# Soft-capped attention into two feed-forward layers on one Trainium2 core: moving the decode of the first weight units behind each pair's reciprocal, two first-half columns first, unread products and another load order in the first pair

## The chip, the cores and the metric

The kernel runs on one core of one Trainium2 chip. The metric is device microseconds of an execution; the time before is 618.9 us, the median of three runs (618.87 to 618.9). About 0.2% of that, 1.2 us, is what a measurement of this kernel can tell from no change.

Engines as the profile names them: PE is TensorE's matmul, PEld its weight load, DVE VectorE, ACT ScalarE, POOL GpSimd, SP SyncE (here it only issues DMAs).

## The reference

```python
scores = cap * np.tanh((1 / np.sqrt(64)) * np.matmul(q, k.transpose(0, 1, 3, 2)) / cap)   # cap = 30
attn = np.exp(scores - np.max(scores, axis=-1, keepdims=True))
attn = attn / (np.sum(attn, axis=-1, keepdims=True) + 1e-09)
x = np.matmul(attn, v)            # 2 batches, 12 heads, 448 tokens, head size 64 -> 896 x 768
h = x @ w_in                      # 768 -> 2048
g = h * (1.0 / (1.0 + np.exp(-1.702 * h)))
x = g @ w_out                     # 2048 -> 768
xn = x / np.sqrt(np.mean(x * x, axis=-1, keepdims=True) + 1e-06) * rms_g
g, val = xn @ w_gate, xn @ w_val  # 768 -> 1536 each
out = (g * (1.0 / (1.0 + np.exp(-g))) * val) @ w_out2
```

All inputs and outputs are float32. The kernel computes the large products with every operand split into a rounded part and a remainder, and three matmuls for each product.

## The kernel before

**Attention.** The 24 heads are worked two at a time, as 12 pairs. `attention()` has a loop over p from 0 to 12 (L436). Iteration p starts the scores of pair p+1 and ends the work of pair p-1, so that three pairs are under way. For a pair PE does seven transposes of q and k (`turn`, L250), the scores in three chunks of 128 keys (`scores`, L292) and a last one of 64 keys for both heads (`scores_last`, L302), the product with v (`outputs`, L324 and L329) and the sums of the exponentials (`sums`, L356). ACT does tanh and exp of each chunk (`exps`, L314 and L315; the last chunk writes `tl`). DVE splits the transposed q and k (`split_kq`, L269 and L270), adds two chunks of exponentials (`add_two`, L343), copies the output `z` (L335), takes the reciprocal of the sums (L361), and, for a pair that is up to four iterations older, multiplies `z` by the spread reciprocal and splits it into the input `x` of the first layer (`normal`, L383, L388, L395). The last pair's copy of `z` and its rounded part are ACT's (L337, L390).

The order on each engine is the order of the code: the program is issued by hand, and an engine works its list from the top. A tile that is used in rotation makes its next writer wait for its last reader. Three things use the two-deep PSUM tile `v` in turn: the last scores chunk of pair p, the outputs of pair p-1, the sums of pair p-1. So the outputs of pair p wait until the reciprocal of pair p-1 has read its sums, and the sums of pair p-1 wait until ACT's tanh of the last chunk of pair p has read that tile.

**First pair.** Six products of ones (L411, `WARM`) run while q and k of the first pair arrive. They are written to a `v` tile that nobody reads. The eight transposes of pair 0 follow (`tq`, `tk`), ACT and DVE split them (L277, L279), and the scores of pair 0 start. SP issues the loads in the order k of pair 0, v of pair 0, k and q of pairs 1 and 2, v of pairs 1 and 2. ACT issues q of pair 0.

**Weights.** The weights come in 68 units of six blocks of 128 x 128 and are loaded as raw words (`load_to`, L113). Each is decoded into a rounded part and a remainder in eight steps: on ACT `square`, `sign`, `mask` (L125, L129, L133), on DVE `mid`, `top`, `low` (L137, L143, L149), then `high_part` on ACT (L158) and `low_part` on DVE (L163, after `high_part`). `low` of a unit also issues the load of the unit three further on. During the attention a table, `plan`, says in which iteration which step of units 0 to 3 is issued. A call in the middle of the iteration issues one ACT step (two in iteration 11). A second call, ahead of `sums`, issues the rest, DVE's among them:

```python
if p >= 4:
    normal(p - 4)
...
decode(p if p < NPR else p + 1)
...
if p >= 1:
    sums(p - 1)
```

**First layer.** `ffn1` computes a column: one weight unit times one of two token ranges, of 384 (`b` = 0) or 512 tokens (`b` = 1), 18 matmuls (L549 to L551). The `b` = 0 columns read only the first batch's pairs, 0 to 5. The `b` = 1 columns read both batches', pair 11 in their last three matmuls. The list `order` starts with `HEAD` = 3 columns of `b` = 0 (units 0, 1, 2), then the same units' `b` = 1. `slots` says which decode steps are issued beside each column. The spread of the last pair's reciprocal (`spread_product`, L376, into `b`) comes behind the first column.

Of the kernel before, what the change touches and what calls it, by code (L numbers as in the profile page):

```python
# [18 lines left out]
def attn_moe_kernel(  # L19
# [157 lines left out]
    def attention():  # L177
        with ExitStack() as actx:
# [66 lines left out]
            def turn(p):  # L245
# [10 lines left out]
                else:  # L256
                    t = [ps_s.tile([128, 2, 512], F32, tag="s", name="tq")[:, 0],
                         ps_t.tile([128, 2, 512], F32, tag="t", name="tk")[:, 0]]
                    for j in range(2):
                        for c in range(NC + 1):  # L260
                            flip(t[j][:, c * 128:(c + 1) * 128], c + (NC if j == 0 else 0))
                turned[p] = t
# [141 lines left out]
            load_v(0)  # L404
            load_k(1)
            load_q(1)
            load_v(1)

            warm = ps_v.tile([128, 512], F32, tag="v", name="v")
            for _ in range(WARM):  # L410
                nc.tensor.matmul(out=warm[:, 0:S], lhsT=ones, rhs=xA[0][:, 0, 0:S], start=True, stop=True)  # L411

            plan = {
                3: [(square, 0)], 4: [(sign, 0)], 5: [(mask, 0)], 6: [(square, 1), (mid, 0)],
                7: [(sign, 1), (top, 0), (low, 0)], 8: [(mask, 1)], 9: [(high_part, 0), (mid, 1)],
                10: [(square, 2), (top, 1), (low_part, 0)], 11: [(sign, 2), (low, 1)],
                12: [(high_part, 1), (mask, 2), (low_part, 1)],
                13: [(square, 3), (sign, 3), (mid, 2)],
                14: [(top, 2), (low, 2)],
                15: [(high_part, 2), (low_part, 2), (mask, 3), (mid, 3), (top, 3), (low, 3)],  # L420
            }

            def decode(p, n=9):
                for _ in range(min(n, len(plan.get(p, ())))):
                    run(*plan[p].pop(0))
# [11 lines left out]
            for p in range(NPR + 1):  # L437
                if p < NPR:
# [9 lines left out]
                    decode(p, 2 if p == NPR - 1 else 1)  # L448
# [7 lines left out]
                if p < NPR:  # L456
                    add_two(p)
                else:
                    decode(NPR)
# [6 lines left out]
                if p == NPR - 1:  # L466
                    late = ps_t.tile([128, 2, 512], F32, tag="t", name="late")
                    spread_product(p - 2, late[:, 0])
                    normal(p - 2)
                decode(p if p < NPR else p + 1)  # L470
# [6 lines left out]
                if p == NPR:  # L477
                    decode(NPR + 2)
                    spread_product(p - 2, late[:, 1])
                    normal(p - 2)  # L480

# [8 lines left out]
            decode(NPR + 3)  # L490
            return spread_product, norm_mul, norm_hi, norm_lo

    def rest(spread_product, norm_mul, norm_hi, norm_lo):
        with ExitStack() as fctx:
# [95 lines left out]
            HEAD = 3  # L590
# [4 lines left out]
            for c in range(NC1):  # L595
# [9 lines left out]
                if c == 0:  # L605
                    slots[0] = [(op, 3) for op in DVE_OPS] + [(op, 4) for op in ACT_OPS] + slots[0]
# [3 lines left out]
                for n, (i, b) in enumerate(order):  # L610
                    last = ()
                    if c == 0 and n == 0:
                        later(lambda: spread_product(q3, bank()))
                        later(*[lambda fn=fn: fn(q3) for fn in (norm_mul, norm_hi, norm_lo)])
                        last = (lambda: load_to(5), load_g, lambda: [run(op, 3) for op in DVE_OPS])
# [243 lines left out]
```

## Time and profile before

| what | value |
|---|---|
| median of three runs | 618.9 us |
| the profiled execution | 618.96 us |
| its span, first to last instruction | 617.2 us |
| PE busy | 605.4 us (98%), 3371 matmuls |
| DVE busy | 450.7 us (73%) |
| ACT busy | 398.7 us (65%) |
| POOL busy | 72.0 us (12%) |

The profiled execution's own time is 1.8 us more than its span; that part is outside the first and last instruction. Busy shares are means over stages that have different limits. The chain that ended last is PE for 93% of the span and DVE for 4%, so what matters is where PE waits, and for whom.

### The profile page before, as it was taken

How to read it: one execution, taken by the hardware profiler on the slowest of the kernel's cores; microseconds unless marked ns; L12 is line 12 of the kernel's file. 1: busy time of each engine (PE TensorE's matmuls, PEld its weight loads, DVE VectorE, ACT ScalarE, POOL GpSimd, SP SyncE). 2: the span in 40 equal slices, each digit the busy share in tenths (PEclk: the TensorE clock that was granted, in tenths of full speed). 3: DMA queues.
4: the chain of work that ended last, by engine and by line, in shares of the span. 5: the costliest groups of instructions: out<-in, count | busy, mean ns of one | idle time of the engine just before them, and what ended most of it. 6: DMA issues, size and time to landing. Idle time of an engine off the chain costs nothing.

```text
span 617.2 us, 8577 instructions
## 1 busy us (share of the span) xinstructions
PE 605.4 (98%) x3371; PEld 515.0 (83%) x3371; DVE 450.7 (73%) x548; ACT 398.7 (65%) x532; POOL 72.0 (12%) x94
## 2 busy tenths in 40 slices
PE   7999998999999999999999999999999999999997
PEld 5555554588888898999888988899988899999997
DVE  1668888869875553666778899997388897688842
ACT  5899989379876465777766675766456574356400
POOL 3232322000000000000022201300022200022100
PEclk9899999999999999999999999999999999999999
DMA  5675541234434323333333432334132343333012
GB/s 134 137 195 134 138 107 30 64 106 150 155 104 152 111 94 103 102 104 102 104 109 112 134 106 103 103 102 154 52 102 103 106 151 104 102 103 103 0 73 107
DMA packets 85079, 67.17 MB, mean 109 GB/s; under 512 B 39040, under 2 KB 82358, under 8 KB 85040
## 3 DMA queue, kind: packets, MB, share of 16 engines
q1 hardware_dynamic: 80448, 64.27, 34.3%
q0 software_dynamic: 3632, 2.13, 1.3%
q8 instruction: 26, 0.43, 0.3%
q10 hardware_dynamic: 960, 0.23, 0.2%
q14 instruction: 13, 0.11, 0.1%
HBM read 63.80 MB, written 2.78 MB: 108 GB/s over the span
## 4 chain that ended last, share of the span: by engine, by line
PE 93%; DVE 4%; issue 1%; DMA 1%; ACT 0%; ACTq 0%; DVEq 0%
PE b L551 22%; PE b L550 22%; PE b L549 22%; PE b L753 14%; PE s L292 4%; PE v L324 4%; PE v L356 2%; PE t L250 1%; PE v L302 1%; PE v L329 1%; DVE rs L361 1%; DMA kq<-in_q 1%; DVE x L269 1%; DVE x L270 1%; DVE z L383 0%
## 5 line engine op out<-in xcount | busy, mean ns | idle before, releaser
L551 PE MATMUL b<-x,ring 128*128 128x512 f32 (+1 forms) x480 | 174.2, 363 | 0.0
L550 PE MATMUL b<-x,ring 128*128 128x512 f32 (+1 forms) x480 | 174.1, 363 | 0.0
L549 PE MATMUL b<-x,ring 128*128 128x512 f32 (+1 forms) x480 | 174.0, 362 | 0.0
L549 PEld LDWEIGHTS b<-x,ring 128*128 128x128 f32 x480 | 90.1, 188 | 10.4 <-issue 0.7
L550 PEld LDWEIGHTS b<-x,ring 128*128 128x128 f32 x480 | 90.1, 188 | 9.8
L551 PEld LDWEIGHTS b<-x,ring 128*128 128x128 f32 x480 | 90.1, 188 | 9.4
L137 DVE SCALAR_TENSOR_TENSOR dec<-raw,dec 128x768 uint32<-128x768 uint32 x68 | 69.7, 1025 | 26.7 <-ACT dec L133 25.3
L753 PE MATMUL b<-ring,uA 128*128 128x384 f32 x504 | 87.8, 334 | 0.0
L753 PEld LDWEIGHTS b<-ring,uA 128*128 128x128 f32 x504 | 87.4, 188 | 0.0
L143 DVE SCALAR_TENSOR_TENSOR dec<-raw,dec 128x768 uint32<-128x768 uint32 x68 | 73.1, 1076 | 1.1
L551 PE MATMUL b<-g,ring 128*128 128x384 f32 (+1 forms) x192 | 70.0, 365 | 0.0
L550 PE MATMUL b<-g,ring 128*128 128x384 f32 (+1 forms) x192 | 69.9, 364 | 0.0
L549 PE MATMUL b<-g,ring 128*128 128x384 f32 (+1 forms) x192 | 69.6, 362 | 0.0
L163 DVE TENSOR_TENSOR ring<-dec,ring 128x768 fp32r<-128x768 f32 x68 | 66.8, 983 | 3.6 <-ACT ring L158 3.6
L158 ACT ACTIVATE ring<-dec 128x768 fp32r<-128x768 f32 x68 | 56.7, 834 | 19.6 <-DVE dec L149 11.4
L149 DVE SCALAR_TENSOR_TENSOR dec<-raw,dec 128x768 uint32<-128x768 uint32 x68 | 64.9, 954 | 1.4
L129 ACT ACTIVATE dec<-dec,edge 128x768 f32<-128x768 f32 x68 | 63.4, 932 | 1.0
L125 ACT ACTIVATE dec<-raw 128x768 f32<-128x768 f32 x68 | 61.0, 896 | 0.6 <-DVE ring L163 0.5
L133 ACT ACTIVATE dec<-dec 128x768 f32<-128x768 f32 x68 | 57.3, 842 | 1.4
L721 POOL TENSOR_TENSOR a<-a,gg 128x512 f32<-128x512 f32 (+1 forms) x18 | 29.6, 1646 | 188.6 <-DVE gg L714 184.2
L724 ACT ACTIVATE uA<-a 128x512 fp32r<-128x512 f32 (+1 forms) x24 | 13.9, 579 | 46.3 <-POOL a L721 34.5
L314 ACT ACTIVATE tt<-s,tsc 128x896 f32<-128x896 f32 x36 | 35.9, 996 | 7.2 <-PE s L292 7.0
(102 smaller groups left out, 675.2 us busy)
## 6 DMA issues: line engine op xcount, KB each, us to landing
raw<-in_moe_w_out SPq DMA_DIRECT2D x20, 768.0 KB, 4.2
raw<-in_moe_w_in SPq DMA_DIRECT2D x16, 768.0 KB, 4.6
raw<-in_moe_w_gate SPq DMA_DIRECT2D x12, 768.0 KB, 4.3
raw<-in_moe_w_val SPq DMA_DIRECT2D x12, 768.0 KB, 4.2
raw<-in_moe_w_out SPq DMA_DIRECT2D x8, 512.0 KB, 3.7
out<-oacc SPq DMA_DIRECT2D x6, 384.0 KB, 2.3
raw<-in_moe_w_out SPq DMA_DIRECT2D x8, 256.0 KB, 3.4
r<-recs POOLq DMA_DIRECT2D x9, 224.0 KB, 7.9
```

The source lines that it names most:

```text
L125: nc.scalar.activation(out=f(d), in_=f(r[:, :, 1]), func=AF.Square, scale=2.0 ** 15)
L129: nc.scalar.activation(out=f(d), in_=f(d), func=AF.Sign, bias=edge)
L133: nc.scalar.activation(out=f(d), in_=f(d), func=AF.Relu, scale=2.0 - 2.0 ** -23)
L137: nc.vector.scalar_tensor_tensor(out=d, in0=hi, scalar=3, in1=d, op0=ALU.logical_shift_left, op1=ALU.bitwise_and)
L143: nc.vector.scalar_tensor_tensor(out=d, in0=hi, scalar=0xC0000000, in1=d, op0=ALU.bitwise_and, op1=ALU.bitwise_or)
L149: nc.vector.scalar_tensor_tensor(out=d, in0=lo, scalar=29, in1=d, op0=ALU.logical_shift_right, op1=ALU.bitwise_or)
L158: nc.scalar.activation(out=t[:, 0], in_=f(dec_t[w][0]), func=AF.Copy)
L163: nc.vector.tensor_tensor(out=t[:, 1], in0=f(d), in1=f(t[:, 0]), op=ALU.subtract)
L549: nc.tensor.matmul(out=wide(o, b), lhsT=w0, rhs=x0, start=first, stop=False)
L550: nc.tensor.matmul(out=wide(o, b), lhsT=w0, rhs=x1, start=False, stop=False)
L551: nc.tensor.matmul(out=wide(o, b), lhsT=w1, rhs=x0, start=False, stop=last)
L753: nc.tensor.matmul(out=os_[t][n][:, 0:HW], lhsT=uA[xi][:, i, tok], rhs=w[:, wi, n * HW:(n + 1) * HW], start=(i == 0 and xi == 0 and wi == ...
```

## The change

Five edits:

1. `plan` becomes `plan_a`, ACT's steps, issued in the middle of an iteration, and `plan_d`, DVE's steps. `plan_d` is issued at the end of the iteration, behind `sums` and so behind the pair's reciprocal.
2. Unit 2 keeps only its three ACT steps in the attention, and these move to iteration 12, beside unit 3's three ACT steps. Its DVE steps and its `high_part` and `low_part` move behind the first column of the first layer (`first`).
3. `HEAD` is 2, so that two columns of `b` = 0 come first instead of three.
4. The unread product of ones is also issued once behind the first transpose of pair 0 and twice behind the last.
5. The loads of k and q of pairs 1 and 2 are issued ahead of the load of v of pair 0.

In iterations 11 and 12, `normal(p - 2)` also moves behind the reciprocal.

```diff
@@ turn(p), for p == 0
                         for c in range(NC + 1):
                             flip(t[j][:, c * 128:(c + 1) * 128], c + (NC if j == 0 else 0))
+                            if j == 0 and c == 0:
+                                warm_up(1)
+                    warm_up(2)
                 turned[p] = t
@@ attention()
-            load_v(0)
             load_k(1)
             load_q(1)
+            load_v(0)
             load_v(1)
...
-            plan = {
-                3: [(square, 0)], 4: [(sign, 0)], 5: [(mask, 0)], 6: [(square, 1), (mid, 0)],
-                7: [(sign, 1), (top, 0), (low, 0)], 8: [(mask, 1)], 9: [(high_part, 0), (mid, 1)],
-                10: [(square, 2), (top, 1), (low_part, 0)], 11: [(sign, 2), (low, 1)],
-                12: [(high_part, 1), (mask, 2), (low_part, 1)],
-                13: [(square, 3), (sign, 3), (mid, 2)],
-                14: [(top, 2), (low, 2)],
-                15: [(high_part, 2), (low_part, 2), (mask, 3), (mid, 3), (top, 3), (low, 3)],
+            def warm_up(times):
+                for _ in range(times):
+                    nc.tensor.matmul(out=warm[:, 0:S], lhsT=ones, rhs=xA[0][:, 0, 0:S], start=True, stop=True)
+
+            warm_up(WARM)
+
+            plan_a = {
+                3: [(square, 0)], 4: [(sign, 0)], 5: [(mask, 0)], 6: [(square, 1)], 7: [(sign, 1)],
+                8: [(mask, 1)], 9: [(high_part, 0)], 11: [(high_part, 1)],
+                12: [(square, 2), (sign, 2), (mask, 2), (square, 3), (sign, 3), (mask, 3)],
             }
+            plan_d = {
+                6: [(mid, 0)], 7: [(top, 0)], 8: [(low, 0)], 9: [(mid, 1)],
+                10: [(top, 1), (low, 1), (low_part, 0)], 11: [(low_part, 1)],
+            }
...
-                    decode(p, 2 if p == NPR - 1 else 1)
+                    decode(plan_a, p)
                     exps(p, 2, s2)
...
                     spread_product(p - 2, late[:, 0])
-                    normal(p - 2)
-                decode(p if p < NPR else p + 1)
                 if p >= 2 and p - 2 < NPR - 3:
                     spread(p - 2)
                 if p >= 1:
...
                 if p == NPR:
-                    decode(NPR + 2)
                     spread_product(p - 2, late[:, 1])
+                if p >= NPR - 1:
                     normal(p - 2)
+                decode(plan_d, p)
@@ rest()
-            HEAD = 3
+            HEAD = 2
...
-                    slots[0] = [(op, 3) for op in DVE_OPS] + [(op, 4) for op in ACT_OPS] + slots[0]
+                    first = (
+                        [(op, 2) for op in (*DVE_OPS, high_part, low_part)]
+                        + [(op, 3) for op in DVE_OPS] + [(op, 4) for op in ACT_OPS] + slots[0]
+                    )
+                    slots[0] = []
...
-                        last = (lambda: load_to(5), load_g, lambda: [run(op, 3) for op in DVE_OPS])
+                        last = (
+                            lambda: [run(*some) for some in first], lambda: load_to(5), load_g,
+                        )
```

Line numbers move in the changed kernel: up to L261 they are the same, then three more (L361 becomes L364), in the first layer's columns five more (L549 becomes L554), and behind them eleven more.

**DVE in iteration 7.** `rs` is the reciprocal's result, `dec` a unit under decoding (here unit 0, `top` at L143 and `low` at L149), `x<-t` the split of the next transposes. Before:

```order
L395 TENSOR_TENSOR x1_67<-z_610,x0_66 128x448
L143 SCALAR_TENSOR_TENSOR dec_478<-raw_372,dec_478 128x768
L149 SCALAR_TENSOR_TENSOR dec_478<-raw_372,dec_478 128x768
L361 RECIPROCAL rs_921<-v_908 128x224
L269 CAST x_961<-t_953 128x896
```

And in the changed kernel:

```order
L398 TENSOR_TENSOR x1_67<-z_613,x0_66 128x448
L364 RECIPROCAL rs_920<-v_907 128x224
L143 SCALAR_TENSOR_TENSOR dec_481<-raw_375,dec_481 128x768
L272 CAST x_961<-t_953 128x896
L273 TENSOR_TENSOR x_961<-t_953,x_961 128x896
```

The two decode steps stood ahead of the reciprocal. Now the reciprocal is first, one decode step follows it, and the other has moved to the next iteration.

**DVE in iterations 10 and 11.** `dec_762` and `dec_765` are unit 1, `ring` the decoded unit; L163 is `low_part` of unit 0. Before:

```order
L395 TENSOR_TENSOR x1_67<-z_890,x0_66 128x448
L143 SCALAR_TENSOR_TENSOR dec_762<-raw_456,dec_762 128x768
L163 TENSOR_TENSOR ring_1036<-dec_478,ring_1036 128x768
L361 RECIPROCAL rs_1176<-v_1163 128x224
L149 SCALAR_TENSOR_TENSOR dec_762<-raw_456,dec_762 128x768
L343 TENSOR_TENSOR ts_1205<-tt_1178,tt_1181 128x896
```

And in the changed kernel:

```order
L398 TENSOR_TENSOR x1_67<-z_893,x0_66 128x448
L364 RECIPROCAL rs_1175<-v_1162 128x224
L143 SCALAR_TENSOR_TENSOR dec_765<-raw_459,dec_765 128x768
L149 SCALAR_TENSOR_TENSOR dec_765<-raw_459,dec_765 128x768
L163 TENSOR_TENSOR ring_1039<-dec_481,ring_1039 128x768
L346 TENSOR_TENSOR ts_1207<-tt_1182,tt_1185 128x896
```

Here too the reciprocal has moved ahead of the decode steps, and three of them now stand between it and the sum of two chunks (`ts`).

**ACT in iteration 11.** `tt` and `tl` are the exponentials of pair 11, and `ring<-dec` is `high_part` of unit 1. Before, behind the first two chunks of the pair:

```order
L129 ACTIVATE dec_1124<-dec_1124,edge_61 128x768
L314 ACTIVATE tt_1195<-s_1184,tsc_60 128x896
L315 ACTIVATE tt_1195<-tt_1195,capt_59 128x896
L314 ACTIVATE tl_1202<-v_1198,tsc_60 128x448
L315 ACTIVATE tl_1202<-tl_1202,capt_59 128x448
L158 ACTIVATE ring_1244<-dec_762 128x768
L133 ACTIVATE dec_1124<-dec_1124 128x768
```

And in the changed kernel:

```order
L158 ACTIVATE ring_1195<-dec_765 128x768
L317 ACTIVATE tt_1197<-s_1188,tsc_60 128x896
L318 ACTIVATE tt_1197<-tt_1197,capt_59 128x896
L317 ACTIVATE tl_1204<-v_1200,tsc_60 128x448
L318 ACTIVATE tl_1204<-tl_1204,capt_59 128x448
L125 ACTIVATE dec_1247<-raw_649 128x768
L129 ACTIVATE dec_1247<-dec_1247,edge_61 128x768
```

Unit 2's `sign` (L129) has gone from this place, and `high_part` of unit 1, which reads what DVE's `low` (L149) of unit 1 writes, now stands ahead of the pair's last two chunks instead of behind them.

## Rows read from the trace of the kernel before

**Rows 1.** The page's first part: busy time, share of the span, instructions of each engine

```profile
PE 605.4 (98%) x3371; PEld 515.0 (83%) x3371; DVE 450.7 (73%) x548; ACT 398.7 (65%) x532; POOL 72.0 (12%) x94
```

**Rows 2.** Windows by stage; behind the window: length, busy us of each engine, PEclk, DMA

```profile
74.00:118.50 44.50, 40.92 (x348) 20.32 (x342) 38.28 (x49) 36.57 (x44) 8.73 (x13) 1.00 0.28 76
140.00:350.00 210.00, 210.00 (x1044) 188.75 (x1044) 145.34 (x172) 148.62 (x213) 9.33 (x8) 1.00 0.37 116
```

**Rows 3.** Waits of PE in the whole span: us in total, times, longest (us)

```profile
PE v L324 <- DVE rs L361: 3.3, 3, 1.9
```

**Rows 4.** Timeline, iterations 7 and 8: start, us, what [idle before <-releaser]

```profile
79.27 0.95 DVE L143 SCALAR_TENSOR_TENSOR dec<-raw,dec 128x768 uint32<-128x768 uint32 x1
...
80.78 0.93 PE L250 MATMUL t<-ident,kq 128*128 128x128 f32 x7
81.14 1.55 DVE L361 RECIPROCAL rs<-v 128x224 f32<-128x224 f32 x1
...
82.74 2.48 PE L324 MATMUL v<-tt,vn 128*64 128x448 f32 x12 [1.03 <-DVE rs L361]
```

**Rows 5.** Timeline of iterations 10 to 12

```profile
98.90 2.48 PE L324 MATMUL v<-tt,vn 128*64 128x448 f32 x12 [0.40 <-DVE rs L361]
...
104.34 0.95 DVE L143 SCALAR_TENSOR_TENSOR dec<-raw,dec 128x768 uint32<-128x768 uint32 x1
...
105.79 0.99 ACT L314 ACTIVATE tt<-s,tsc 128x896 f32<-128x896 f32 x1
106.08 1.55 DVE L361 RECIPROCAL rs<-v 128x224 f32<-128x224 f32 x1
...
107.68 2.48 PE L324 MATMUL v<-tt,vn 128*64 128x448 f32 x12 [1.87 <-DVE rs L361]
107.75 0.62 ACT L314 ACTIVATE tl<-v,tsc 128x448 f32<-128x448 f32 x1
...
108.98 0.83 ACT L158 ACTIVATE ring<-dec 128x768 fp32r<-128x768 f32 x1
...
111.60 0.58 PE L356 MATMUL v<-ts,ones 128*32 128x224 f32 x8
...
116.37 0.59 PE L356 MATMUL v<-ts,ones 128*32 128x224 f32 x8 [0.27 <-DVE rs L361]
...
118.55 0.44 PE L549 MATMUL b<-x,ring 128*128 128x384 f32 x1
```

**Rows 6.** Timeline, PE alone, from the first product to the transposes of pair 3

```profile
1.57 2.61 PE L411 MATMUL v<-x,ones 128*128 128x448 f32 x6 [1.57 <-DVE x L399]
...
4.94 1.42 PE L250 MATMUL tq<-ident,kq 128*128 128x128 f32 x3 [0.55 <-DMA kq<-in_q]
...
7.84 4.08 PE L292 MATMUL s<-x,x 64*128 64x448 f32 x18 [0.63 <-ACT x L277]
...
13.13 1.40 PE L250 MATMUL t<-ident,kq 128*128 128x128 f32 x7
15.81 0.47 PE L292 MATMUL s<-x 64*128 64x448 f32 x2 [1.28 <-DVE x L269]
...
17.45 1.73 PE L250 MATMUL t<-ident,kq 128*128 128x128 f32 x7
...
23.21 0.93 PE L250 MATMUL t<-ident,kq 128*128 128x128 f32 x7
```

**Rows 7.** One window of one microsecond, columns as in Rows 2

```profile
20.00:21.00 1.00, 1.00 (x8) 0.88 (x6) 0.97 (x2) 0.36 (x1) 0.00 (x0) 0.53 0.35 79
```

**Rows 8.** Timeline, ACT: the two waits of pair 1

```profile
17.57 1.01 ACT L314 ACTIVATE tt<-s,tsc 128x896 f32<-128x896 f32 x1 [0.95 <-PE s L292]
...
20.64 1.01 ACT L314 ACTIVATE tt<-s,tsc 128x896 f32<-128x896 f32 x1 [0.99 <-PE s L292]
```

**Rows 9.** Timeline: the first column's way to the decode of unit 3

```profile
128.79 0.58 ACT L390 ACTIVATE x<-z 128x448 fp32r<-128x448 f32 x1 [4.29 <-DVE z L383]
...
131.25 0.52 ACT L578 ACTIVATE g<-gg 128x384 fp32r<-128x384 f32 x1
```

More of the change, by code (lines that the diff above doesn't have):

```diff
@@ L403, in attention, with decode @@
             constants()
-            load_v(0)
             load_k(1)
             load_q(1)
+            load_v(0)
             load_v(1)
             warm = ps_v.tile([128, 512], F32, tag="v", name="v")
-            for _ in range(WARM):
-                nc.tensor.matmul(out=warm[:, 0:S], lhsT=ones, rhs=xA[0][:, 0, 0:S], start=True, stop=True)
-            plan = {
-                3: [(square, 0)], 4: [(sign, 0)], 5: [(mask, 0)], 6: [(square, 1), (mid, 0)],
-                7: [(sign, 1), (top, 0), (low, 0)], 8: [(mask, 1)], 9: [(high_part, 0), (mid, 1)],
-                10: [(square, 2), (top, 1), (low_part, 0)], 11: [(sign, 2), (low, 1)],
-                12: [(high_part, 1), (mask, 2), (low_part, 1)],
-                13: [(square, 3), (sign, 3), (mid, 2)],
-                14: [(top, 2), (low, 2)],
-                15: [(high_part, 2), (low_part, 2), (mask, 3), (mid, 3), (top, 3), (low, 3)],
-            }
-            def decode(p, n=9):
-                for _ in range(min(n, len(plan.get(p, ())))):
-                    run(*plan[p].pop(0))
+            def warm_up(times):
[6 more added lines that the diff above has]
+                12: [(square, 2), (sign, 2), (mask, 2), (square, 3), (sign, 3), (mask, 3)],
+            }
+            plan_d = {
+                6: [(mid, 0)], 7: [(top, 0)], 8: [(low, 0)], 9: [(mid, 1)],
+                10: [(top, 1), (low, 1), (low_part, 0)], 11: [(low_part, 1)],
+            }
+            def decode(plan, p):
+                for op in plan.get(p, ()):
+                    run(*op)
             def normal(p):
@@ L458, in attention @@
                 else:
-                    decode(NPR)
+                    decode(plan_a, p)
                 if p >= 1:
@@ L489, in attention @@
                     load_to((1, 2, 4).index(p))
-            decode(NPR + 3)
             return spread_product, norm_mul, norm_hi, norm_lo
```

## The prediction

> **What bounds the kernel now.** I read the page's busy times first, then windows by stage, PE's waits, the timelines around these waits, and last the opening, where the clock is not steady. PE is busy for 605.4 of 617.2 us [rows 1], so about 12 us are all that waiting can give back; more can come only from products that run at the lower clock. By stage, PE is busy for all 210 us of the window in the feed-forward layers, and for 40.92 of 44.50 us in the second half of the attention [rows 2]: 3.58 us are lost there, at a granted clock of 1.00. PE's waits name the place: three times, 3.3 us in all, the outputs wait for DVE's reciprocal [rows 3]. The timelines show these one by one, 1.03, 0.40 and 1.87 us, and a fourth of 0.27 us in front of the last sums [rows 4, 5]. Their sum is 3.57 us, which is the whole loss of the stage. The reader should see in rows 4 why: two decode steps run on DVE from 79.27 on, the reciprocal starts only at 81.14, and the outputs that need its tile at 82.74.
>
> In the opening ACT is what the first pairs turn on, and it waits for PE's scores twice, 0.95 and 0.99 us [rows 8]. PE is late there because its products are slow. Seven transposes take 1.40 us at 13.13, 1.73 us at 17.45 and 0.93 us at 23.21 [rows 6]. The granted clock averages 0.53 in the microsecond from 20 to 21 [rows 7]: the lower level, 1.2 GHz, until about 20.9, then 2.4 GHz. The first rows' clock reads 1.00, but their durations say otherwise: 18 scores take 4.08 us. So I take the lower level from the start to about 14 us, the upper one for the products at 15.81, and the lower one again from about 17.5. Ahead of that fall PE had idled behind DVE's split, 1.28 us the first time [rows 6].
>
> **The change part by part.** All sums are against the profiled execution, 618.96 us; the median of the runs is 0.06 us less.
>
> *Decode behind the reciprocal, iterations 6 to 9.* Nothing is added. With the reciprocal in the place of the first step it starts at 79.27 and ends near 80.8. The outputs, without their wait of 1.03, would start at 82.74 - 1.03 = 81.71, so the wait goes whole. What is late next? One decode step of 0.95 us behind the reciprocal ends near 81.8, and the split of the next transposes can't start before these end, 80.78 + 0.93 = 81.71 [rows 4]. One step fits; a second would not, and the table has just one in each of these iterations. So 1.03 + 0.40 = **1.43 us** are gained by 98.90 [rows 4, 5].
>
> *Iterations 10 and 11.* In iteration 10 DVE was free for the reciprocal at 104.34; 1.43 earlier is 102.91, and it ends 1.55 later, at 104.46. The outputs would be ready at 107.68 - 1.87 - 1.43 = 104.38, and start, 0.05 behind the reciprocal as before, at 104.51: **0.13 us** of wait stay. Behind the reciprocal come two steps of unit 1, which end near 106.4. Now ACT: `high_part` of unit 1 stands ahead of the last two chunks of pair 11 and reads the second of these steps. Before, it ran behind them, at 108.98 [rows 5]. From 106.4 it takes 0.83, the tanh of the third chunk starts near 107.2, that of the last chunk 1.96 later (105.79 to 107.75) at 109.2, and ends at 109.8. That frees the `v` tile that the sums of pair 10 write. They came 3.92 us behind the outputs (107.68 to 111.60), so they would be ready at 108.43 and wait to 109.8: **a new wait of 1.4 us** that no row of before shows. It is at least 0, if the step is done earlier than I put it, and at most about 1.9, if DVE is half a microsecond later. The wait of 0.27 in front of the last sums goes, since the reciprocal behind the late sums ends near 112.6 and these sums come at 114.3; `normal(p - 2)`, now behind the reciprocal, has no reader before the first `b` = 1 column. The stage gains 3.57 - 0.13 - 1.4 = **2.0 us**; bounds 1.5 and 3.4. The first column starts near 116.5 instead of 118.55.
>
> *Unit 2 decoded later, two columns first.* No step is added. Unit 2 was wanted third and is now wanted fifth, and the `b` = 1 columns start one column sooner. A unit's two columns are 36 matmuls, and 1044 take 210 us [rows 2]: 7.2 us, by their widths 3.1 for `b` = 0 and 4.1 for `b` = 1. The spread takes about 0.9 of the 2.18 us from the last sums to the first column [rows 5]. So column 5 starts at 116.5 + 2 x 3.1 + 0.9 + 2 x 4.1 = 131.8 and the first column of unit 3 at 131.8 + 3.1 + 4.1 = 139.0. The first gate chain sits on ACT behind the last pair's `x`: from the start of that to the end of `high` it takes 131.77 - 128.79 = 2.98 us [rows 9]. The spread ends near 116.5 + 3.1 + 0.9 = 120.5, the multiply 0.6 later, the chain at 124.1, and DVE's subtraction at 124.7. Unit 2 then takes three steps of 0.98, ACT's copy of 0.83 and a subtraction of 0.95: ready at 129.4, 2.4 us ahead. Unit 3 has three DVE steps to 132.3 and ACT's copy; four DVE instructions of other work and its own subtraction follow: ready near 137, 2.0 us ahead. So I cost these edits at **nothing**, hidden behind the columns. If that cover is gone, each microsecond beyond it is one of PE. Pair 11's `x` is wanted behind 15 matmuls of the third column, near 127, and is there near 122.5.
>
> *Unread products.* One runs in the wait behind the first transpose, two between the last transpose and the scores, where PE was idle for 0.63 [rows 6]. At the lower level two take about 0.8 us (six took 2.61 [rows 6]), so they push the scores by at most 0.2; I take 0, because ACT's split is what the scores wait for. What they may bring is the clock. Ahead of the rise near 14 PE had been at work without a gap since 7.84, ahead of that at 20.9 since 17.45 [rows 6]. Now unbroken work starts at 4.94 instead of 7.84. I put the rise earlier by as much, 2.9 us, near 11; the early bound is the first score. ACT's chain of pair 0 stays as it was and leaves ACT free at 17.57 - 0.95 = 16.62. At the upper level from 11 on, the rest of pair 0's scores and the transposes end near 12.9, DVE's split, two steps of 1.1 us, near 15.1, and the scores that ACT then wants near 15.7; the next ones follow by 17.3. Both waits go, 0.95 + 0.99 = **1.94 us** [rows 8]. At the early bound the first scores too are done about 0.5 sooner: 2.5. If the clock stays as it was: 0, or a loss of 0.2.
>
> *Load order.* With PE two microseconds earlier at the second transposes, k and q of pairs 1 and 2 must be there. SP issues its list one by one, and their eight DMAs now stand ahead of five others instead of behind them. Alone this is worth 0: PE had no wait at 13.13 [rows 6]. v of pair 0 is issued eight DMAs later, but its outputs come only behind the transposes at 23.21 [rows 6].
>
> Sum: 618.96 - 2.0 - 1.94 = 615.0; the median 0.06 lower, **614.9**.
>
> The Trainium skill, "TensorE: Matmul & The Clock Gate" (What's actually happening), says that the point at which the clock rises is not set by the kernel's start and differs from run to run, so that one kernel shows different numbers of slow products. Here three runs lie within 0.03 us of each other, which speaks for a rise at the same point each time.
>
> **Rivals.**
>
> *The clock does not gain.* The three products don't raise it sooner. For it: transposes fill much of the time ahead of 7.84, and the clock did not rise during them. Then only the 2.0 us remain: 616.9.
>
> *The clock falls later.* It rises early, PE then idles behind DVE's split and ACT, as it did ahead of 17.5, and a slow stretch like that from 17.5 to 20.9 falls into the pairs that run back to back: half of its 3.4 us, 1.7, is lost again. Against it: the wait of 1.87 us did not lower the clock [rows 2, 5]. Result 616.6.
>
> *No wait on ACT.* The sums of pair 10 are not held: 3.4 + 1.94, 613.6.
>
> *A wandering clock.* The rise comes at another point in each run: then the runs spread from 614.4 to 616.9, a median near 615.6. This is the rule of the Trainium skill above, on the page named there.
>
> *Slower: the decode is late in the first layer.* Units 2 and 3 now stand behind the first gate chain. With 2.0 us of extra lateness PE begins to wait, at 2.0 + 4.0 = 6.0 us the kernel is no faster than before, and with 9 us it takes 618.96 + 3.0 = 622.0. For it: ACT and DVE each wait for the other three times in a unit. Against it: the durations above, and PE's unbroken 210 us with the same steps [rows 2].
>
> **How the numbers follow.** Chances: forecast 0.5, clock does not gain 0.2, clock falls later 0.12, no wait on ACT 0.1, wandering clock 0.05, slower 0.03. The likeliest gives 614.9. The low end takes both large bounds, 3.4 and 2.5: 613.1. The high end is the forecast's 2.0 without any gain in the opening and a loss of 0.2 there: 617.1. The bound of what can be told from no change is 0.2%, 1.2 us; all cases but the last gain more in their middle, and the lower bound of the stage, 1.5, without the opening comes near it. So faster 0.92, same 0.05, slower 0.03.
>
> **What would show it.** PE's list of waits has the outputs behind the reciprocal for under 0.3 us in all. A wait of the sums for ACT's tanh of the last chunk appears once, 1 to 1.9 us, near the end of the attention. ACT's two waits of rows 8 are gone, and the first seven-transpose group behind the scores takes about 0.9 us instead of 1.40. The first column starts near 114.5 in the new span. PE is busy throughout behind it. The prediction is wrong if the clock still reads the lower level near 18 to 21 us, if the sums don't wait, or if PE waits for `ring` in the first ten columns.

## The result and the profile after

The changed kernel takes **614.34 us** (median of six runs, 614.18 to 614.6), the kernel before 618.9 (six runs beside them, 618.64 to 621.24): a ratio of 0.992, 95% interval 0.9905 to 0.9934. The forecast was 614.9, its range 613.1 to 617.1. The profiled execution took 614.47 us, span 612.7; the span is 4.5 us shorter.

The page's first part and then PE's waits (us in total, times, longest) of the changed kernel, against [rows 1] and [rows 3]:

```profile
PE 603.5 (99%) x3374; PEld 513.2 (84%) x3374; DVE 450.7 (74%) x548; ACT 398.6 (65%) x532; POOL 72.0 (12%) x94
```

```profile
PE s L295 <- ACT tt L317: 1.6, 2, 1.1
PE v L416 <- DVE x L402: 1.6, 1, 1.6
PE s L295 <- DVE x L272: 1.3, 1, 1.3
PE s L295 <- DVE x L273: 0.6, 1, 0.6
PE tq L250 <- DMA kq<-in_q: 0.2, 1, 0.2
PE v L359 <- DVE z L338: 0.2, 1, 0.2
```

PE is busy 1.9 us less, though it issues three more products, and idles 2.6 us less; together they are the 4.5. The outputs' waits for the reciprocal, 3.3 us before, have left the list; a gap of 0.13 us in iteration 10 is too short to be listed. The sums wait once, 0.2 us, for DVE's copy and not for ACT.

The opening, PE's timeline (start, us, what, idle before and its releaser), against [rows 6]:

```profile
7.82 3.46 PE L295 MATMUL s<-x,x 64*128 64x448 f32 x18
...
11.93 0.93 PE L250 MATMUL t<-ident,kq 128*128 128x128 f32 x7
14.13 0.47 PE L295 MATMUL s<-x 64*128 64x448 f32 x2 [1.28 <-DVE x L272]
...
15.77 0.98 PE L250 MATMUL t<-ident,kq 128*128 128x128 f32 x7
...
19.52 0.88 PE L295 MATMUL s<-x 64*128 64x448 f32 x6 [1.09 <-ACT tt L317]
...
21.89 2.48 PE L327 MATMUL v<-tt,vn 128*64 128x448 f32 x12
```

The scores take 3.46 instead of 4.08, the transposes behind them 0.93 instead of 1.40: the lower level (1.2 GHz) ends within the scores, near 10.5, and does not come back. Now it is PE that waits for ACT.

The middle, from iteration 9 on, PE's timeline and then ACT's, against [rows 4, 5]:

```profile
94.31 0.88 PE L295 MATMUL s<-x 64*128 64x448 f32 x6 [0.49 <-ACT tt L317]
...
102.97 2.48 PE L327 MATMUL v<-tt,vn 128*64 128x448 f32 x12
...
107.18 0.59 PE L359 MATMUL v<-ts,ones 128*32 128x224 f32 x8 [0.22 <-DVE z L338]
...
108.45 2.48 PE L327 MATMUL v<-tt,vn 128*64 128x448 f32 x12
...
113.79 0.44 PE L554 MATMUL b<-x,ring 128*128 128x384 f32 x1
...
117.27 0.98 PE L379 MATMUL b<-rs,sel 128*64 128x224 f32 x8
```

```profile
87.35 0.84 ACT L158 ACTIVATE ring<-dec 128x768 fp32r<-128x768 f32 x1 [1.69 <-DVE dec L149]
...
104.75 0.84 ACT L158 ACTIVATE ring<-dec 128x768 fp32r<-128x768 f32 x1 [2.28 <-DVE dec L149]
105.50 0.99 ACT L317 ACTIVATE tt<-s,tsc 128x896 f32<-128x896 f32 x1
...
107.47 0.61 ACT L317 ACTIVATE tl<-v,tsc 128x448 f32<-128x448 f32 x1
```

`high_part` of both units (L158) waits on ACT for DVE's `low`, 1.69 and 2.28 us, and the exponentials queue behind it. The sums start at 107.18, before ACT's tanh of the last chunk (107.47 to 108.08) has read its tile, so that is not the tile they write.

Where the 4.5 us come from is read by marks, the starts of the same work in the two traces, each of one execution:

| mark | before | after | gain so far | forecast so far |
|---|---|---|---|---|
| outputs of pair 0 | 24.07 | 21.89 | 2.18 | 1.94 |
| outputs of pair 3 | 48.73 | 46.58 | 2.15 | 1.94 |
| outputs of pair 7 [rows 4] | 82.74 | 79.49 | 3.25 | 2.97 |
| outputs of pair 9 | 98.90 | 95.93 | 2.97 | 3.37 |
| outputs of pair 10 | 107.68 | 102.97 | 4.71 | 5.11 |
| outputs of pair 11 | 112.87 | 108.45 | 4.42 | 3.71 |
| first column | 118.55 | 113.79 | 4.76 | 3.98 |
| spread behind it | 121.87 | 117.27 | 4.60 | 3.98 |

Behind that no wait of PE is listed, and in the window of the feed-forward layers PE is busy throughout (second line, columns as in [rows 2]). The window ahead of it (first line) has 0.84 us of idle time where there were 3.58:

```profile
72.00:116.00 44.00, 43.16 (x359) 22.45 (x356) 38.58 (x50) 37.53 (x44) 9.34 (x15) 1.00 0.29 79
140.00:350.00 210.00, 210.00 (x1048) 189.15 (x1047) 146.14 (x173) 147.59 (x213) 10.37 (x9) 1.00 0.37 116
```

### The profile page after: what moved, and what is told of

The parts are those of the page before. It is cut to its first block, busy times and chain, and to the rows that moved or that the text cites. A ratio compares the mean times of both kernels' runs of the same rounds, so it can differ in the third digit from the quotient of the medians.

```text
span 612.7 us, 8578 instructions
## 1 busy us (share of the span) xinstructions
PE 603.5 (99%) x3374; PEld 513.2 (84%) x3374; DVE 450.7 (74%) x548; ACT 398.6 (65%) x532; POOL 72.0 (12%) x94
## 4 chain that ended last, share of the span: by engine, by line
PE 85%; DMA 10%; ACT 2%; DVE 1%; issue 1%; POOL 1%; ACTq 0%; POOLq 0%
PE b L556 22%; PE b L555 22%; PE b L554 22%; PE b L764 14%; DMA recs<-rs 9%; DMA r<-recs 1%; PE s L295 1%; PE v L327 1%; ACT tt L317 1%; POOL r L374 1%; ACT tt L318 1%; PE v L359 1%; DVE rs L364 1%; DMA kq<-in_q 1%; PE v L305 0%
## 5 line engine op out<-in xcount | busy, mean ns | idle before, releaser
L554 PE MATMUL b<-x,ring 128*128 128x512 f32 (+1 forms) x480 | 174.0, 362 | 0.0
L554 PEld LDWEIGHTS b<-x,ring 128*128 128x128 f32 x480 | 90.1, 188 | 10.4 <-issue 0.7
L143 DVE SCALAR_TENSOR_TENSOR dec<-raw,dec 128x768 uint32<-128x768 uint32 x68 | 73.1, 1075 | 1.1
L158 ACT ACTIVATE ring<-dec 128x768 fp32r<-128x768 f32 x68 | 56.7, 834 | 23.9 <-DVE dec L149 15.6
L163 DVE TENSOR_TENSOR ring<-dec,ring 128x768 fp32r<-128x768 f32 x68 | 66.8, 984 | 4.5 <-ACT ring L158 4.5
L554 PE MATMUL b<-g,ring 128*128 128x384 f32 (+1 forms) x192 | 69.6, 362 | 0.0
L149 DVE SCALAR_TENSOR_TENSOR dec<-raw,dec 128x768 uint32<-128x768 uint32 x68 | 64.9, 954 | 1.5
L129 ACT ACTIVATE dec<-dec,edge 128x768 f32<-128x768 f32 x68 | 63.3, 932 | 1.0
L555 PEld LDWEIGHTS b<-g,ring 128*128 128x128 f32 x192 | 36.0, 188 | 4.0
```

What stands on the lines that cost most here:

```text
L129: nc.scalar.activation(out=f(d), in_=f(d), func=AF.Sign, bias=edge)
L143: nc.vector.scalar_tensor_tensor(out=d, in0=hi, scalar=0xC0000000, in1=d, op0=ALU.bitwise_and, op1=ALU.bitwise_or)
L149: nc.vector.scalar_tensor_tensor(out=d, in0=lo, scalar=29, in1=d, op0=ALU.logical_shift_right, op1=ALU.bitwise_or)
L158: nc.scalar.activation(out=t[:, 0], in_=f(dec_t[w][0]), func=AF.Copy)
L163: nc.vector.tensor_tensor(out=t[:, 1], in0=f(d), in1=f(t[:, 0]), op=ALU.subtract)
L554: nc.tensor.matmul(out=wide(o, b), lhsT=w0, rhs=x0, start=first, stop=False)
```

## The experiments

Twelve measurements of ten kernels and of two repeats, in three groups that each shared the runs of the kernel before (medians 618.65, 618.87, 618.68). Unless said otherwise each is the changed kernel with one edit, and the ratio is against the kernel before.

**The parts of the opening.** First without both of its edits (`a_old_start`):

```diff
-                            if j == 0 and c == 0:
-                                warm_up(1)
-                    warm_up(2)
...
+            load_v(0)
             load_k(1)
             load_q(1)
-            load_v(0)
```

> The changed kernel without the three unread products and with the loads in the old order; the decode order and the two columns first stay. Theory (the opening and the second half of the attention gain apart from each other, 2.2 and 2.3 us): 616.5 us, 616.2 to 616.8; the first outputs start near 24.1 us as before and the granted clock reads 0.50 between 18 and 20 us. Rival (the opening gain is given back later, or comes from the decode order): 614.3 us.

Measured: 615.8 (614.95 to 616.35), ratio 0.9961, 0.9947 to 0.9974: slower than the changed kernel, by less than forecast. The two signs of the theory did not show in the profiled execution (615.17 us): its outputs of pair 0 start at 22.25, not near 24.1, and the granted clock reads 1.00 between 18 and 20. Then the first half of that diff alone (`a_no_products`):

> The changed kernel without the three unread products, with the new load order. Theory (the products raise the clock, the load order alone is worth nothing): 616.5 us, 616.2 to 616.8, 18 scores of pair 0 in about 4.1 us. Rival (the earlier loads alone bring the second transposes forward): about 615.4 us.

Measured: 615.39 (614.71 to 616.45), ratio 0.9957, 0.9942 to 0.9972; three of six runs within 0.12 us of 614.72, three at 615.96 to 616.45. The median is the rival's number, but it lies between the two sets of runs. The profiled execution, one of the quicker three, has the outputs of pair 0 at 21.87, as early as the changed kernel with its products (21.89). And the second half alone (`a_old_loads`):

> The changed kernel with the three products, loads in the old order. Theory (the clock gains, but q of pair 1 lands near 13.5 us, so the second transposes wait about 1 us from 12 us on, and ACT then waits for pair 1's scores for a part of it): 614.6 to 615.3 us. Rival A (the order is worth nothing, ACT covers the wait): 614.3 us. Rival B (the wait lowers the clock again and the opening gain goes): 616 us or more.

Measured: 615.79 (615.16 to 617.08), ratio 0.9964, 0.995 to 0.9978, between the theory's 615.3 and rival B's 616. Last, the other way round: the kernel before with the products and the load order of the change, and nothing else (`b_new_start`).

> The kernel before with the unread products and the load order of the change alone; decode and columns as before. Theory (the opening is worth 1.2 to 2.2 us by itself, whatever stands behind it): 617.0, range 616.6 to 617.5. Rival (the opening's gain is given back behind it, at the first weight load or at the reciprocals, when the decode stands ahead of them): 618.3 to 618.9.

Measured: 617.2 (616.63 to 620.46, 12 runs), ratio 0.9992, 0.9977 to 1.0008: by the interval it can't be told from no change, since its runs scatter and those of the kernel before too. Those came out, in this group of 28, at 617.0 to 617.7 ten times and at 618.5 to 621.1 the rest. The mean granted clock is 1.000 in each of those ten and 0.992 to 0.997 in the other eighteen (3.4 us at 0.50, as in the profiled execution, take 0.003 off the mean). So the kernel before reaches 617.0 to 617.7 by itself where the clock does not fall, and its profiled execution, 618.96, is one in which it does. The profile of `b_new_start` (616.99 us) shows one thing more: its marks are ahead of before's by 1.98 us at the outputs of pair 0, 1.96 at pair 7 and 1.97 at the first column. What that execution gains in the opening is kept, whatever stands behind it; there the rival falls.

So the opening is worth 1.2 to 1.5 us by the medians (615.8 against 614.34 and 614.58; 618.68 against 617.2), less than the 2.18 by which the two profiled executions differ, and either edit alone leaves 615.4 or 615.8. That it needs both is likely rather than shown: the changed kernel ran in other groups than these three, and the intervals of the ratios overlap; but eleven of its twelve runs are at most 614.78, and only three of the twelve with one edit are as low as 614.83. What the old loads cost shows in the timeline of the kernel with the products and the old loads, and in its windows:

```profile
11.98 1.25 PE L250 MATMUL t<-ident,kq 128*128 128x128 f32 x6
13.76 0.33 PE L250 MATMUL t<-ident,kq 128*128 128x128 f32 x1 [0.53 <-DMA kq<-in_q]
15.37 0.47 PE L295 MATMUL s<-x 64*128 64x448 f32 x2 [1.27 <-DVE x L272]
```

```profile
18.00:19.00 1.00, 1.00 (x7) 0.63 (x7) 0.53 (x1) 0.97 (x2) 0.00 (x0) 0.50 0.41 93
19.00:20.00 1.00, 1.00 (x8) 0.90 (x6) 0.97 (x2) 0.30 (x2) 0.00 (x0) 0.50 0.57 130
```

PE is early enough to find that q of the next pair has not landed. It waits 0.53 us and starts the scores 1.24 us later than in the changed kernel (15.37 against 14.13); in this execution the granted clock also fell to 0.50, and the outputs of pair 0 came at 23.34 instead of 21.89.

**The decode behind the reciprocal.** The DVE steps put ahead of the sums again, all else as changed (`a_old_place`):

```diff
+                decode(plan_d, p)
                 if p >= 2 and p - 2 < NPR - 3:
                     spread(p - 2)
...
-                decode(plan_d, p)
```

> The changed kernel with its DVE decode steps issued ahead of the sums and their reciprocal, as before, in the new table's iterations. Theory (what stands ahead of the reciprocal delays the outputs): three steps in iteration 10 cost 1.87 + 0.95 - 0.13 = 2.7 us, one step in iteration 9 costs 0.4, one in 7 about 0.1: 617.5 us, 616.9 to 618.0. Rival (the table's iterations bring the gain, the place does not): 614.3 us.

Measured: 618.5 (616.63 to 619.47, 12 runs), ratio 1.0003, 0.9992 to 1.0013: the whole gain is gone, 1.0 us more than the expectation took from it. PE's waits, and DVE's timeline in iteration 10:

```profile
PE v L327 <- DVE rs L364: 3.3, 2, 2.8
```

```profile
100.93 0.95 DVE L143 SCALAR_TENSOR_TENSOR dec<-raw,dec 128x768 uint32<-128x768 uint32 x1
101.92 0.96 DVE L149 SCALAR_TENSOR_TENSOR dec<-raw,dec 128x768 uint32<-128x768 uint32 x1
102.80 0.95 DVE L163 TENSOR_TENSOR ring<-dec,ring 128x768 fp32r<-128x768 f32 x1
103.66 1.55 DVE L364 RECIPROCAL rs<-v 128x224 f32<-128x224 f32 x1
```

Three steps stand ahead of the reciprocal, and the outputs of pair 10 come 9.77 us behind those of pair 9 instead of 7.04: 2.73 us, as the expectation had it. What it had not: in the next iteration `low_part` of unit 1 stands ahead of the reciprocal of pair 10 as well, and the step to pair 11 grows from 5.48 to 6.52.

The stage can be told from the opening by the time from the outputs of pair 3 to the first column. It is 69.82 us before and 69.81 in `b_new_start`; 67.18 to 67.24 in the changed kernel, its repeat, the three kernels with another opening and `a_head3`, however their clock moved; and 70.93 in `a_old_place`. So the new decode is worth 2.6 us there, and the new table with the old place is worse than the old table. No run has the new place with unit 2's decode left in the attention, so what edit 2 adds to edit 1 is not shown.

**Two columns first.** `HEAD = 2` back to `HEAD = 3`, with unit 2 decoded late as in the change (`a_head3`):

> The changed kernel with three columns of the first batch first, as before, and unit 2's decode still behind the first column. Theory (the two columns are what hides the later decode): unit 2 is wanted near 121.3 us of the span and its rounded part is there near 126.7, its remainder near 127.6, so PE waits 5.4 to 6.2 us: 619.7 to 620.6 us. Rival (the banks and ACT's backlog let PE run on, or the decode is early enough): 614.3 us.

Measured: 622.81 (622.07 to 622.84), ratio 1.0064, 1.0052 to 1.0076. The wait is there, but the price is higher than the wait. PE's waits, and windows around it:

```profile
PE b L554 <- ACT ring L158: 5.1, 1, 5.1
```

```profile
126.00:128.00 2.00, 1.26 (x3) 0.77 (x4) 1.28 (x2) 1.97 (x3) 0.00 (x0) 0.53 0.39 69
128.00:132.00 4.00, 4.00 (x13) 4.00 (x14) 3.90 (x5) 2.74 (x4) 0.00 (x0) 0.50 0.52 176
132.00:134.00 2.00, 2.00 (x9) 1.83 (x9) 1.97 (x4) 1.95 (x4) 0.00 (x0) 0.77 0.93 280
```

Behind 5.08 us without work PE comes back at a granted clock of 0.50, the lower level, until about 133, and the third column takes 6.25 us (126.74 to 132.99) where unit 2's takes 3.15 in the changed kernel. The wait of 5.1 and the 3.1 of this column are the 8.2 us to 614.58. So the decode of unit 2 can be late only because two columns come first; the two edits belong together.

**The new wait on ACT.** `high_part` of both units one iteration later, and `low_part` of unit 1 with it (`a_late_copies`):

```diff
-                8: [(mask, 1)], 9: [(high_part, 0)], 11: [(high_part, 1)],
-                12: [(square, 2), (sign, 2), (mask, 2), (square, 3), (sign, 3), (mask, 3)],
+                8: [(mask, 1)], 10: [(high_part, 0)],
+                12: [(high_part, 1), (square, 2), (sign, 2), (mask, 2), (square, 3), (sign, 3), (mask, 3)],
...
-                10: [(top, 1), (low, 1), (low_part, 0)], 11: [(low_part, 1)],
+                10: [(top, 1), (low, 1), (low_part, 0)], 12: [(low_part, 1)],
```

> The changed kernel with high_part of units 0 and 1 one iteration later, so that ACT no longer waits for DVE's low ahead of a chunk, and low_part of unit 1 in iteration 12. Theory (the spread of the last pair waits for its reciprocal, which stands behind normal of pair 8 and that behind its reciprocal's DMA): ACT's waits of 1.7 and 2.3 us and PE's of 0.5 us go, but the first column but one starts no earlier: 614.3 us, within 0.3. Rival (the waits on ACT are what is left): 613.7 us.

Measured: 615.2 (614.41 to 615.99), ratio 0.9946, 0.9933 to 0.9958; the changed kernel, run beside it, follows below. Both numbers of the expectation were missed. The waits it names went: the step from the outputs of pair 8 to those of pair 9 is 7.46 us instead of 8.21, that from pair 10 to 11 is 5.19 instead of 5.48, and the first column came at 112.97. Then PE waited for two other things:

```profile
PE b L556 <- DVE ring L163: 0.8, 1, 0.8
...
PE b L379 <- DVE rs L364: 0.4, 1, 0.4
```

Both are DVE's: it waits for the broadcast reciprocal of pair 8 to come back by DMA before `normal(8)`, and the last reciprocal and `low_part` of unit 1 stand behind that. They give back what the first column had won; what else is in the 615.2 its profile does not show. In the changed kernel the same queue costs the 0.16 us at the spread (DVE's timeline):

```profile
114.03 0.62 DVE L386 TENSOR_TENSOR z<-z,r 128x448 f32<-128x448 f32 x1 [1.39 <-DMA r<-recs]
...
115.67 1.55 DVE L364 RECIPROCAL rs<-v 128x224 f32<-128x224 f32 x1
```

So the next kernel also puts the last reciprocal ahead of `normal(8)` (`a_late_copies_recip`):

```diff
-                if p >= 4:
+                if 4 <= p < NPR:
                     normal(p - 4)
...
                     spread_product(p - 2, late[:, 1])
+                if p == NPR:
+                    normal(p - 4)
```

> The same, and in iteration 12 the last reciprocal ahead of normal of pair 8. Theory: the spread no longer waits for the DMA's result, and the 0.5 us of the waits and 0.2 us of the spread come out: 613.6 us, 613.3 to 613.9, the spread into b starts 0.7 us earlier relative to the first outputs. Rival (normal of pair 8 then holds up the columns that read it, or the spread waits elsewhere): 614.3 us.

Measured: **613.96** (613.69 to 614.23), ratio 0.9925, 0.9913 to 0.9937, just above the theory's range, and a second time (`a_recip_again`):

> The changed kernel with the three decode copies later and the last reciprocal ahead of normal(8), once more, beside the kernel with the early first weight load. Theory: 613.96 as in the first measurement, within 0.3 us, and 0.4 to 0.8 us above the kernel with the early load. Rival: the two are the same within 0.3 us.

Measured: **613.65** (613.52 to 614.38), ratio 0.9925, 0.9905 to 0.9945. It is the fastest kernel here, 0.6 us below the changed one in the group that had both (613.96 against 614.58). The intervals of their ratios overlap, but nine of its eleven runs lie below all twelve of the changed kernel. What PE still waits for behind the opening is the reciprocal, 0.16 us at the outputs of pair 10, and `low_part` of unit 1, 0.45 us in the second column.

**The changed kernel once more** (`after_again`).

> The changed kernel itself, beside the next three on one chip. Theory (the point at which the clock rises differs from run to run, and the three products with the new load order make the opening nearly independent of it): 614.3 us with its own runs less than 1 us apart, while the runs of the kernel before are spread over 2 us. Rival (the products only shift the point): the runs are spread as far as those of the kernel before.

Measured: 614.58, ratio 0.9943, 0.9925 to 0.996. Five runs lie between 614.21 and 614.78, one at 617.3; the kernel before gave 617.27 to 619.11 beside it. By their range these runs are spread as far as the rival says; without the one, which no trace explains, as the theory says.

**The first weight load.** In runs in which the scores ran at the upper level from their first product, part of the gain was lost again by pair 3. ACT's timeline of the kernel with the late copies and the early reciprocal:

```profile
37.56 0.92 ACT L125 ACTIVATE dec<-raw 128x768 f32<-128x768 f32 x1 [1.92 <-DMA raw<-in_moe_w_in]
```

ACT's first decode step waits for the first weight unit, and the exponentials queue behind it. In the changed kernel that wait was 0.73 us. The edit, on top of the fastest kernel, issues the load one iteration earlier (`a_early_raw`):

```diff
-                if p in (1, 2, 4):
-                    load_to((1, 2, 4).index(p))
+                if p in (0, 2, 4):
+                    load_to((0, 2, 4).index(p))
```

> The changed kernel with the three decode copies later and the last reciprocal ahead of normal(8), and in addition the load of the first weight unit issued at the end of iteration 0 instead of 1. Theory (an early rise of the clock is given back because ACT's square of unit 0 waits for its load, 0.7 us in the changed kernel and 1.9 us in a run whose clock rose early): the wait goes, the outputs of pairs 0 to 4 follow each other at 8.22 us each, and the time is near 613.3, range 613.0 to 613.8. Rival (the load is hidden anyway, or pushes the k and q of the next pairs back by as much): 613.96, as without this edit.

Measured: 615.65 (614.44 to 617.55, 11 runs), ratio 0.9954, 0.9939 to 0.9969: 2.0 us slower than without the edit, where 0.4 to 0.8 faster was expected. Its ACT and then its PE:

```profile
35.62 0.87 ACT L125 ACTIVATE dec<-raw 128x768 f32<-128x768 f32 x1
```

```profile
59.07 0.96 PE L332 MATMUL v<-tl,ve 128*64 128x448 f32 x2 [1.62 <-DMA ve<-in_v]
```

The theory's own steps hold: ACT does not wait, and the outputs of pairs 0 to 4 follow each other at 8.22 us (21.33 to 54.22). But those of pair 5 come 10.81 us later, because PE finds v of pair 4 not there. SP's list issued that load 3.5 us later than in the kernel without the edit (timelines of SP, this kernel and then `a_recip_again`):

```profile
45.46 5.49 SPq L235 DMA_DIRECT2D vn<-in_v  x3
51.04 1.30 SPq L239 DMA_DIRECT2D ve<-in_v  x2
```

```profile
45.17 2.27 SPq L235 DMA_DIRECT2D vn<-in_v  x3
47.53 2.09 SPq L239 DMA_DIRECT2D ve<-in_v  x2
```

Why SP's list stood still there, 3.1 us of it put down to PE's scores, is not settled. The next kernel, which has this edit too, waits for the same load, 1.5 us.

**More products.** On top of that, three unread products (`warm_up(3)`) behind pair 1's transposes (`a_filled`):

> The kernel with the early first weight load, and three more unread products of ones behind pair 1's seven transposes, where PE idles 1.28 us for DVE's split. Theory (the idle time of PE in the opening is what lets the clock fall back there): no stretch at the lower clock between 14 and 21 us, and 613.0, range 612.6 to 613.4. Rival (the clock's moves there do not turn on this idle time): a slow stretch is still seen, or the time stays at that of the kernel without the products, and the products may cost up to 0.3 us.

Measured: 616.25 (615.16 to 617.46, 12 runs), ratio 0.9963, 0.9949 to 0.9978: no faster, as the rival has it. In its profile the clock did not fall between 14 and 21 us, but the outputs of pair 0 came at 21.11, only 0.22 us ahead of the 21.33 of `a_early_raw`, in which it did fall: there ACT is the bound (in this profile busy for 0.97 us or more of each microsecond from 9 to 22).

## Why the prediction was right, and where it was not

**What bounds the kernel: right.** The waits of the outputs for the reciprocal were the loss of the stage. They are gone but for 0.13 us, and `a_old_place`, with the steps ahead of the reciprocal again, has 3.3 us of them and no gain left. The stage as a whole gave 2.6 us where 2.0 were forecast.

**Iterations 6 to 9: right in the part named, 0.7 us short beside it.** The 1.03 us came as forecast (the gain grows from 2.15 to 3.25). The 0.40 of pair 9 came too, but was more than taken back: the gain falls to 2.97 instead of growing to 3.37. The step that failed is "one step fits", which looked at DVE alone. `low` of unit 0 had moved from iteration 7 to 8, and ACT's `high_part`, in the same place as before, now waits for it, 1.69 us; PE shows 0.49 of that as a wait. `a_late_copies`, which moves `high_part` on, has the 0.7 us back. A rotation of the decode has two engines, and the prediction followed one.

**Iteration 10: right.** 1.74 us were forecast between the outputs of pairs 9 and 10, 1.74 came, and the 0.13 that stay are where they were put: the outputs start at 102.97, 0.06 behind the end of the reciprocal and 0.13 behind that of PE's product before.

```profile
101.36 1.55 DVE L364 RECIPROCAL rs<-v 128x224 f32<-128x224 f32 x1
...
101.96 0.88 PE L305 MATMUL v<-x,kb 128*128 128x448 f32 x3
```

**The wait of the sums: wrong, 1.4 us for ACT forecast, 0.22 for DVE measured.** ACT's chain came as worked out: `high_part`, tanh of the third chunk, tanh of the last. But "that frees the `v` tile that the sums of pair 10 write" was wrong: they start at 107.18, ahead of the tanh that was to free it, and what they wait for is DVE's copy of the outputs of pair 10. So they write the tile of those outputs. The wait for ACT's tanh, 1 to 1.9 us, that the prediction named as a sign did not appear. The prediction, and the description of the kernel before with it, took the two-deep rotation as strict, because in the trace of before no wait told which of the two tiles it is. This was also priced as a rival, "no wait on ACT" (613.6); with the 0.7 us lost in iteration 9 the result came out between that and the forecast.

**Behind the attention.** The wait of the last sums goes (+0.34 at the first column, 0.27 forecast). Unforeseen are 0.16 us at the spread, which waits for the last reciprocal behind `normal(8)`. In the sum: 3.98 forecast by marks (1.94 + 3.57 - 0.13 - 1.40, which the text rounded to 3.94), +0.21 in the opening, +0.07 up to pair 7, -0.68 up to pair 9, +1.11 at the sums, +0.07 and -0.16 behind, is the 4.60 of the table. Two errors of opposite sign, -0.68 and +1.11, nearly cancelled, so that the total came as near as it did is in part luck.

**Unit 2 late, two columns first: right at nothing.** DVE's timeline in the changed kernel, the end of units 2 and 3:

```profile
126.69 0.96 DVE L163 TENSOR_TENSOR ring<-dec,ring 128x768 fp32r<-128x768 f32 x1 [0.91 <-ACT ring L158]
...
133.75 0.95 DVE L163 TENSOR_TENSOR ring<-dec,ring 128x768 fp32r<-128x768 f32 x1
```

Unit 2 is ready at 127.65 and its first column starts at 129.62, 2.0 us later (2.4 forecast); unit 3 is ready at 134.70, some 2 us ahead of its own. The slower rival, decode too late, needed 2.0 us of lateness that never came. `a_head3` shows what lies beyond the margin, and that the rival's price there was too low: lost cover also lowers the clock.

**The opening: the place was right, 2.18 against 1.94, the reading of the clock wrong.** ACT's two waits of [rows 8] are gone. The forecast rise near 11 was right for this execution. But 2.18 is the difference of two executions; by the medians the term is 1.2 to 1.5. And the rise is no fixed point. In the eleven profiles with the products it comes within the scores of pair 0 or ahead of them; in the three without them, before, `a_old_start` and `a_no_products`, only behind them or at their end. How early it comes changes from run to run. Pair 0's first scores (18 or 12 products, as the view merges them), in three kernels that have the same program up to there:

```profile
7.97 3.70 PE L295 MATMUL s<-x,x 64*128 64x448 f32 x18
```

```profile
7.85 2.18 PE L295 MATMUL s<-x,x 64*128 64x448 f32 x12
```

```profile
7.71 1.75 PE L295 MATMUL s<-x,x 64*128 64x448 f32 x12
```

The first is the changed kernel again, the others those with the late copies, without and with the early reciprocal. 1.75 us for twelve is the upper level from the first score on. The Trainium skill, "TensorE: Matmul & The Clock Gate" (What's actually happening), says just this, and the prediction set it aside on three runs that lay within 0.03 us of each other. Those three were too few: later runs of the same kernel lie between 617.0 and 621.2. What kept the forecast right, as far as the eleven profiles tell, is that with the products late rises are rare, and that the early ones bring little more: ACT is the bound behind them, and its wait for the first weight load takes most of the rest. The outputs of pair 0 lie at 20.76 us in `a_old_place` and at 21.89 in the changed kernel; those of pair 3 at 46.20 and 46.58. So of that rival, a wandering clock, the mechanism is shown, while its spread of 2.5 us and its median of 615.6 did not come: eleven of the changed kernel's twelve runs lie between 614.18 and 614.78. Against the rival that the clock does not gain stand the medians, 614.34 and 614.58 with the opening and 615.8 without it; the mark of pair 0 does not decide it, as `a_no_products` reached the same one. A later fall was seen in other kernels, not in the profiles of the changed one.

**Load order alone: right at 0, incomplete.** Alone it is worth 0.4 us at most by the medians (615.39 against 615.8), but without it the products brought nothing (615.79).

## What to carry to other kernels

When a step moves, follow its reader on the other engine to the place where that stands: here the gain on DVE was partly paid on ACT, in a queue in front of the exponentials. Where a wait depends on which of two tiles a writer gets, and no row tells, take both cases to the sum as equals. Each load at the start is a place in SP's list: in `a_early_raw` one moved forward, a load that the edit did not name came 3.5 us later, and the kernel lost 2.0 us; by what steps was not traced.

## What the runs showed of the hardware

- TensorE's clock does not rise at a fixed time of the program. Of fourteen profiles, the first scores show it up from their first product in six. A single profile of an opening, or three equal times, say little; the medians of 5 to 28 runs were needed. The 28 runs of the kernel before in the last group fall into ten of 617.0 to 617.7 us, all at a mean granted clock of 1.000, and eighteen of 618.5 us or more, all at 0.992 to 0.997.
- It fell back between 15 and 21 us in six of the fourteen, behind idle times of some 1.27 and 0.56 us that were the same in all but one of those in which it did not (`a_filled`, 0.66 and 0.57). `a_early_raw` (fell, 0.50 from 16 to 18 us) and `a_recip_again` (did not, 1.00 in the same stretch) run the same program up to there. Behind 5.08 us of idle time (`a_head3`) it had fallen in the one profile there is.
- A reciprocal sent out and back through DRAM for its broadcast takes about 7 us out and 8.6 back (98.14 to 105.1 and 105.39 to 114.01 for pair 8). In the changed kernel this chain, and not PE, sets the last reciprocal.
